# Fewer, larger transposes, one normalisation and a regrouped output projection in a decode attention kernel for two caches

## The chip, the cores and the metric

The kernel runs on one core of one Trainium2 chip. A time is device time of one execution in microseconds (us). The span of a profile runs from the first to the last instruction and is about 1.8 us shorter than the time. The kernel before takes 2564.32 us (median of 3 runs, 2564.31 to 2564.78).

## The reference, cut to what matters

Two independent attention layers, A and B, each decode one token for 8 sequences with 32 heads of 128. Everything is bf16.

```python
B, Sq, D = 8, 1, 1024
H, Sk, Dh = 32, 4096, 128
q = (x @ wq)...                                  # (B, H, 1, Dh)
scores = einsum("bhqd,bhkd->bhqk", q, k_cache) * Dh ** -0.5
o = einsum("bhqk,bhkd->bhqd", softmax(scores), v_cache)
out = o... @ wo                                  # (B, 1, D); A and B side by side
```

Each query meets its own keys and values once, so every byte of the caches is used in one small product. Each of the four caches has 268 MB, and each of the four weight matrices 8.4 MB.

## The kernel before

One tile is 8 heads of one sequence: 128 partitions of 64 KB, 8.39 MB. There are 132 of them: 64 of keys, 64 of values, two of wq and two of wo. They go through a ring of three buffers, all on SyncE's queue:

```python
plan = [("wq", 0, 1), ("k", 0, 0), ("wq", 1, 2)]          # kind, number, buffer
for n in range(NQ - 1):
    plan.append(("k", n + 1, (n + 1) % 2))
    plan.append(("v", n, 2))
plan += [("v", NQ - 1, NQ % 2), ("wo", 0, 2), ("wo", 1, (NQ - 1) % 2)]
```

For every key tile VectorE multiplies by the query (four pieces) and folds, TensorE and VectorE finish the sums, ScalarE makes the exponentials, VectorE spreads them into `PM`, and TensorE multiplies `PM` by the value tile.

The head of the kernel computes q. ScalarE copies eight pieces of it out of PSUM; they are transposed in four rounds of 8 rows, and each round is copied by VectorE:

```python
for hb in range(HB):                                      # 4 rounds
    rows = slice(32 * hb, 32 * hb + B)
    def emit(e, rows=rows):
        for j in range(HQ):
            i = e.transpose(misc_bf16[:, j * B:(j + 1) * B], q_sb[rows, c, j * Dh:(j + 1) * Dh], ident[rows, rows],
                            tile_position=(rows.start, 0))
        return i
    op = add("pe", emit, [opQs[(c, hb, 0)], opQs[(c, hb, 1)], ...])
    ... = add("dve", lambda e, hb=hb: e.tensor_copy(qT..., misc_bf16...), [op])
```

The tail multiplies by wo. The second wo comes in four pieces, so that TensorE can begin before the last has landed:

```python
wo_cuts = ((0, 12), (12, 24), (24, H - 2), (H - 2, H))    # rows r of the second wo
nt = NT if c == NC - 1 else NT // 2                       # column tiles: 2 of 512 for A, 4 of 256 for B
...
for r in range(r0, r1):
    for q in range(nt):
        col = r * D + q * dt
        x = e.matmul(proj[32 * q:32 * q + B, 0:dt], on_sb[:, c, r, :], w[:, col:col + dt],
                     start=(r == 0), stop=(r == H - 1), tile_position=(0, 32 * q))
...
opEv[c] = add("dve", lambda e: e.tensor_copy(orow[0:rows, 0:dt], proj[0:rows, 0:dt]), [opProj[c]] + outs)
for q in range(nt):                                       # B: four stores, two on each of two queues
    outs.append(dma(out[:, 0, c * D + q * dt:c * D + (q + 1) * dt], orow[32 * q:32 * q + B, 0:dt],
                    ("out", 0), [opEv[c]], "sp" if q % 2 == 0 else "act"))
```

Of the kernel before, what the change touches and what calls it, by code (L numbers as in the profile page):

```python
# [4 lines left out]
ACTF = mybir.ActivationFunctionType  # L5
ALU = mybir.AluOpType
AX = mybir.AxisListType
BF16 = mybir.dt.bfloat16
FP32 = mybir.dt.float32
# [130 lines left out]
def _build_kernel(nc, caches, out):  # L140
    B, Sq, D = caches[0][0].shape
    _, H, Sk, Dh = caches[0][1].shape
    NC = len(caches)
# [3 lines left out]
    HQ = 8  # L147
# [7 lines left out]
    RG = T // 4 // 4  # L155
    PH = 128 // H
    MB = HQ * PH
    NT = 4
    DT = D // NT

    es = ExitStack()
    with es:
# [19 lines left out]
        PM = sb("PM", [128, T, HQ], BF16)  # L182
        accS = sb("accS", [128, 512], BF16)
        o_sb = sb("o_sb", [128, NC * B * H], FP32)
        rl = sb("rl", [128, B], FP32)
        on_sb = sb("on_sb", [128, NC, H, B], BF16)
        orow = sb("orow", [128, 2 * DT], BF16)
        q_sb = PM[:].rearrange("p t j -> p (t j)").rearrange("p (c n) -> p c n", c=NC)

        red_ps = [ps(f"red{i}", 16 * CT) for i in range(2)]  # L190
# [4 lines left out]
        q_ps = [o_ps, pv_ps]  # L195
        misc_bf16 = misc.bitcast(BF16)

        wo_cuts = ((0, 12), (12, 24), (24, H - 2), (H - 2, H))
        sems = {e: es.enter_context(nc.semaphore(f"c_{e}")) for e in ENGINES[1:]}
        for name, n in (("t", 3), ("w", len(wo_cuts)), ("x", 1), ("out", 1)):  # L200
            for i in range(n):
# [5 lines left out]
        def dma(out_ap, in_ap, key, deps, eng="sp"):  # L207
            return add(eng, lambda e: e.dma_start(out_ap, in_ap), deps, dma_key=key)
# [10 lines left out]
        c_own = pool_select(own_m[:], MP - 1, [[MP, HQ], [0, PH]], c_own, ALU.is_ge, 0.0, -1)  # L219
        own = own_m[:, :, 0]  # L220

        c_E = add("pool", lambda e: e.memset(E[:], 0.0))
        for q in range(4):
            c_E = pool_select(E[:, :, PH - 1:].rearrange("p i (j u) -> p i j u", u=PH)[:, :, :, 0], -32 * q, [[-8, 4], [-1, HQ]], c_E)
        c_oh = add("dve", lambda e: e.tensor_copy(own_h[:], own), [c_own])
        c_half = add("dve", lambda e: e.tensor_reduce(half[:], own.rearrange("p (g i) -> p i g", i=2), AX.X, ALU.add), [c_own])
        c_half = add("dve", lambda e: e.tensor_scalar(half[:], half[:], 1e30, -1e30, ALU.mult, ALU.add), [c_half])
        c_proj = add("dve", lambda e: e.memset(proj[:], 0.0))

        opT, opMul, opEacc, opRed, opNgm, opExp = {}, {}, {}, {}, {}, {}  # L230
        opPV, opAcc, opExt, opSt, opQb, opQbc, opQ, opQs, opQT = {}, {}, {}, {}, {}, {}, {}, {}, {}
# [24 lines left out]
        def load_tiles():  # L256
            while issued[0] < len(plan):
                kind, n, w = plan[issued[0]]
                prev = before[issued[0]]
                dep = opUse.get(prev)  # L260
                if prev is not None and dep is None:
                    return
                to, key = ring[:, w, :], ("t", w)
                if kind in ("k", "v"):
                    c, b, hb = where(n)
                    from_ = caches[c][1 if kind == "k" else 2][b, hb * HQ:(hb + 1) * HQ].rearrange("u (m t) d -> (u m) (t d)", m=MP)
                    opT[(kind, n)] = dma(to, from_, key, [dep])
                elif kind == "wq":
                    opT[(kind, n)] = dma(to[:, 0:DC * H * Dh], caches[n][3].rearrange("(p k) n -> p (k n)", k=DC), key, [dep])
                else:  # L270
                    from_ = caches[n][4].rearrange("(p r) n -> p (r n)", r=H)
                    for i, (r0, r1) in enumerate(wo_cuts if n == NC - 1 else ((0, H),)):
                        opT[(kind, n, i)] = dma(to[:, r0 * D:r1 * D], from_[:, r0 * D:r1 * D], key if n < NC - 1 else ("w", i), [dep])
                issued[0] += 1


        def make_q(c):
            w = tile_of("wq", c)
            for f in range(2):
                def emit(e, f=f):  # L280
                    for k in range(DC):
                        for hb in range(HB):
                            col = k * H * Dh + (2 * hb + f) * 512
                            i = e.matmul(q_ps[f][32 * hb:32 * hb + B, :], xT[:, (c * DC + k) * B:(c * DC + k + 1) * B],
                                         w[:, col:col + 512], start=(k == 0), stop=(k == DC - 1), tile_position=(0, 32 * hb))
                    return i
                opQ[(c, f)] = add("pe", emit, [c_xT, opT[("wq", c)]] + [opQs.get((c - 1, hb, f)) for hb in range(HB)])
                for hb in range(HB):
                    rows = slice(32 * hb, 32 * hb + B)
                    opQs[(c, hb, f)] = add("act", lambda e, rows=rows, f=f: e.activation(q_sb[rows, c, f * 512:(f + 1) * 512], q_ps[f][rows, :], ACTF.Copy),  # L290
                                           [opQ[(c, f)]])
            opUse[("wq", c)] = opQ[(c, 1)]

        def make_qT(c):
            for hb in range(HB):
                rows = slice(32 * hb, 32 * hb + B)

                def emit(e, rows=rows):
                    for j in range(HQ):
                        i = e.transpose(misc_bf16[:, j * B:(j + 1) * B], q_sb[rows, c, j * Dh:(j + 1) * Dh], ident[rows, rows],  # L300
                                        tile_position=(rows.start, 0))
                    return i
                op = add("pe", emit, [opQs[(c, hb, 0)], opQs[(c, hb, 1)], c_ident, c_xT, opQT.get("last"), opQbc.get(0), opQbc.get(1)])
                opQT[c] = opQT["last"] = add("dve", lambda e, hb=hb: e.tensor_copy(  # L304
                    qT[:, c].rearrange("p (b h) -> p h b", h=H)[:, hb * HQ:(hb + 1) * HQ, :],
                    misc_bf16[:, 0:HQ * B].rearrange("p (j b) -> p j b", b=B)), [op])

        def make_stage(n):
            def emit(e, at):
# [95 lines left out]
                          [opExt[n]], moves=True)  # L405


        def make_norm(c):
            ns = range(c * HB * B, (c + 1) * HB * B)

            def emit(e):
                for hb in range(HB):
                    x = e.matmul(misc[MB * hb:MB * (hb + 1), 0:B], own_m[:].rearrange("p j u -> p (j u)"),
                                 rsum[:].rearrange("p (n h) -> p h n", h=HB)[:, hb, c * B:(c + 1) * B], start=True, stop=True, tile_position=(0, MB * hb))
                return x
            ls = add("pe", emit, [opExp[ns[-1]], c_own, opQbc[NQ - 1], opNorm.get(c - 1)])
            rec = add("dve", lambda e: e.reciprocal(rl[:], misc[:, 0:B]), [ls, opNorm.get(c - 1)])
            opNorm[c] = add("dve", lambda e: e.tensor_tensor(
                on_sb[:, c].rearrange("p r b -> p b r"), o_sb[:, c * B * H:(c + 1) * B * H].rearrange("p (b r) -> p b r", b=B),
                rl[:].unsqueeze(2).to_broadcast([128, B, H]), ALU.mult), [rec, opOc[ns[-1]]])  # L420

        def make_proj(c):
            w = tile_of("wo", c)

            nt = NT if c == NC - 1 else NT // 2
            dt = D // nt
            for i, (r0, r1) in enumerate(wo_cuts if c == NC - 1 else ((0, H),)):
                def emit(e, r0=r0, r1=r1):
                    for r in range(r0, r1):
                        for q in range(nt):  # L430
                            col = r * D + q * dt
                            x = e.matmul(proj[32 * q:32 * q + B, 0:dt], on_sb[:, c, r, :], w[:, col:col + dt],  # L432
                                         start=(r == 0), stop=(r == H - 1), tile_position=(0, 32 * q))
                    return x
                opProj[c] = add("pe", emit, [opNorm[c], opT[("wo", c, i)], c_proj, opEv.get(c - 1)])
            rows = 32 * (nt - 1) + B
            opEv[c] = add("dve", lambda e: e.tensor_copy(orow[0:rows, 0:dt], proj[0:rows, 0:dt]), [opProj[c]] + outs)  # L437
            for q in range(nt):
                outs.append(dma(out[:, 0, c * D + q * dt:c * D + (q + 1) * dt], orow[32 * q:32 * q + B, 0:dt],
                                ("out", 0), [opEv[c]], "sp" if q % 2 == 0 else "act"))  # L440


        x_sb = ring[0:B, 2, 0:NC * D].rearrange("p (c d) -> p c d", c=NC)
        op_x = [dma(x_sb[:, c, :], caches[c][0].rearrange("b s d -> b (s d)"), ("x", 0), [c_oh], "act") for c in range(NC)]

        def emit_xT(e):
            for c in range(NC):
                for k in range(DC):
                    col = (c * DC + k) * B
                    i = e.transpose(misc_bf16[:, col:col + B], x_sb[:, c, :].rearrange("b (p k) -> b k p", k=DC)[:, k, :],  # L450
                                    ident[0:B, 0:B])
            return i
        op_xT = opUse[("x", 0)] = add("pe", emit_xT, [c_ident, op_x[-1]])
        load_tiles()
# [37 lines left out]
        make_red(NS - 1)  # L492
        make_shift(n)
        make_pm(n)
        make_norm(0)
        make_pv(n, 0, RG)
        make_acc(n)
        load_tiles()
        make_ext(n)
        make_norm(1)  # L500
        make_proj(0)
        make_proj(1)
        assert issued[0] == len(plan)
# [3 lines left out]
            o.token = (("x", 0), 16 * NC)  # L507
        loops = {"pe": (1, 2, (NQ - 2) // 2), "dve": (3, 2, (NQ - 4) // 2), "act": (3, HB, (NQ - 4) // HB)}

        P.run("sp", nc.sync, sems, part=(0, 2))  # L510
        block = es.enter_context(nc.Block())

        @block.sync
        def _(eng):
            P.run("sp", eng, sems, part=(2, None))
            eng.wait_ge(sems[("out", 0)], counts[("out", 0)])

        @block.tensor
        def _(eng):
# [10 lines left out]
        @block.gpsimd  # L530
        def _(eng):
            P.run("pool", eng, sems)


def bass_concat_heads__mha_block_cached__mha_block_cached__decode_kernel(
# [32 lines left out]
```

## Time and profile before

| what | before |
|---|---|
| time, median of 3 | 2564.32 us |
| span of the profile | 2563.2 us |
| bytes moved | 1107.49 MB |
| busy: TensorE, VectorE, ScalarE | 44%, 85%, 5% |

These are lines of the page. The rows of digits show the busy share of 40 slices of the span, in tenths; the line after the rate is the chain of waits that ended last, by engine; the last line is the costliest group of VectorE, where the figures after the bar are busy time, mean ns of one instruction, and idle time before them with what ended it.

```profile
span 2563.2 us, 18707 instructions
PE 1122.2 (44%) x7648; PEld 395.1 (15%) x7648; DVE 2173.1 (85%) x1043; ACT 130.0 (5%) x401; POOL 2.6 (0%) x14
...
DVE  3898898898898898898898888888988988988983
...
DMA  9999999999999999999999999999999999999999
...
HBM read 1107.33 MB, written 0.03 MB: 432 GB/s over the span
...
DMA 52%; DVE 28%; issue 16%; PE 4%; another core or an unknown queue 0%; ACT 0%; DVEq 0%; SPq 0%
...
L329 DVE TENSOR_TENSOR ring<-ring,qbc 128x8192 bf16<-128x8192 bf16 x256 | 1131.8, 4421 | 311.3 <-DMA ring<-in_A_k_cache_dram 153.5
```

The DMA row shows 9, 90% or more, in all 40 slices: the load stream runs through, at 432 GB/s over the span. VectorE is nearly as busy, and the chain of waits spends 28% on it, but it waits 311.3 us in all for key tiles: 4.9 us for each of 64.

The head, from the timeline: start, duration, engine, operation, and in brackets the idle time before it and what ended that. "SPq" and "ACTq" lines are DMA issues.

```profile
1.27 0.42 SPq L208 DMA_DIRECT2D ring<-in_A_k_cache_dram  x1
...
2.29 0.17 DVE L225 CAST own_h<-own_m 128x8 bf16<-128x8 f32 x1 [2.29 <-POOL own_m L212]
...
3.12 0.29 ACTq L208 DMA_DIRECT2D ring<-in_B_x_dram  x1
...
29.31 2.43 ACT L290 ACTIVATE PM<-pv 8x512 bf16<-8x512 f32 x4
...
29.95 0.35 PE L300 MATMUL misc<-ident,PM 8*128 8x8 bf16 x8 [0.92 <-ACT PM L290]
30.34 0.43 DVE L304 COPY qT<-misc 128x64 bf16<-128x64 bf16 x1 [13.00 <-PE misc L300]
...
33.24 0.43 DVE L304 COPY qT<-misc 128x64 bf16<-128x64 bf16 x1 [0.53 <-PE misc L300]
...
34.40 0.28 ACT L318 ACTIVATE qbc<-misc 128x128 bf16<-128x128 f32 x1 [0.38 <-PE misc L316]
...
43.72 4.42 DVE L329 TENSOR_TENSOR ring<-ring,qbc 128x8192 bf16<-128x8192 bf16 x1 [10.04 <-DMA ring<-in_A_k_cache_dram]
```

The first query is ready at 34.68 us, and VectorE then waits until 43.7 us for the first key tile. The first rounds of transposes start at 29.95.

The tail, from the timeline:

```profile
2549.49 1.48 PE L432 MATMUL proj<-ring,on_sb 128*8 128x256 bf16 x48 [0.78 <-DVE orow L437]
2555.12 2.73 PE L432 MATMUL proj<-ring,on_sb 128*8 128x256 bf16 x48 [4.14 <-DMA ring<-in_B_wo_dram]
2558.61 1.88 PE L432 MATMUL proj<-ring,on_sb 128*8 128x256 bf16 x32 [0.76 <-DMA ring<-in_B_wo_dram]
2560.54 0.42 DVE L437 CAST orow<-proj 104x256 bf16<-104x256 f32 x1 [11.11 <-PE proj L432]
2560.99 0.63 SPq L208 DMA_DIRECT2D out_dram<-orow  x2
```

One stretch of it by window; after the busy times come TensorE's granted clock, the DMA share and the rate:

```profile
2558.00:2560.00 2.00, 1.39 (x28) 0.78 (x32) 0.00 (x0) 0.00 (x0) 0.00 (x0) 0.50 0.25 100
```

The clock is at half here. TensorE had idled 4.14 us between the first two pieces of the second wo, and in that time the clock fell: it was 1.00 from 2545 to 2552 us and from 2553.0 to 2553.5, and 0.50 from 2554 us on. The same 48 matmuls took 1.48 us in the first piece and 2.73 us in the second. The last piece landed at 2559.8 us, and 3.4 us later the kernel ended.

### The profile page before, as it was taken

What the parts mean: (1) busy time and instruction counts of PE and PEld (TensorE: products, weight loads), DVE (VectorE), ACT (ScalarE), POOL (GpSimd) and SP (SyncE); (2) the same over time, 40 slices, a digit from 0 to 9 for tenths busy, and PEclk for the clock granted to TensorE, in tenths of its full rate; (3) what the DMA queues carried; (4) which work ended last, traced back from release to release, by engine and by line L of the source; (5) the groups of instructions that cost most, each with busy time, mean ns of one, the idle gap of its engine ahead of it and who ended that gap; (6) DMA issues with size and microseconds to landing.
All of it is one profiled execution on the core that took longest, in us unless ns stands there. A gap on an engine that the chain in (4) does not pass through costs nothing.

```text
span 2563.2 us, 18707 instructions
## 1 busy us (share of the span) xinstructions
PE 1122.2 (44%) x7648; PEld 395.1 (15%) x7648; DVE 2173.1 (85%) x1043; ACT 130.0 (5%) x401; POOL 2.6 (0%) x14
## 2 busy tenths in 40 slices
PE   2443443443444444444444444443434444434435
PEld 1111111111111111111111111111111111111112
DVE  3898898898898898898898888888988988988983
ACT  1100000000000000000000000000000000000000
POOL 0000000000000000000000000000000000000000
PEclk7666675766667676766767666767767667666667
DMA  9999999999999999999999999999999999999999
GB/s 425 427 438 430 437 431 437 431 437 431 436 432 436 431 437 430 438 430 438 430 438 429 438 430 438 429 437 431 437 431 436 432 436 432 434 433 434 433 435 391
DMA packets 19577, 1107.49 MB, mean 432 GB/s; under 512 B 2224, under 2 KB 2272, under 8 KB 2416
## 3 DMA queue, kind: packets, MB, share of 16 engines
q1 hardware_dynamic: 19488, 1107.32, 99.9%
q8 instruction: 6, 0.10, 0.0%
q10 hardware_dynamic: 80, 0.05, 0.0%
q14 instruction: 3, 0.02, 0.0%
HBM read 1107.33 MB, written 0.03 MB: 432 GB/s over the span
## 4 chain that ended last, share of the span: by engine, by line
DMA 52%; DVE 28%; issue 16%; PE 4%; another core or an unknown queue 0%; ACT 0%; DVEq 0%; SPq 0%
DMA ring<-in_A_k_cache_dram 25%; DMA ring<-in_B_k_cache_dram 25%; DVE ring L329 10%; DVE ring L334 10%; PE red L344 4%; DVE s_sb L352 4%; DVE PM L369 3%; DMA ring<-in_B_wo_dram 1%; DVE rmax L358 1%; DVE rtmp L359 0%; ACT PM L290 0%; DVEq L135 0%; DVE ngm L362 0%; PE proj L432 0%
## 5 line engine op out<-in xcount | busy, mean ns | idle before, releaser
L329 DVE TENSOR_TENSOR ring<-ring,qbc 128x8192 bf16<-128x8192 bf16 x256 | 1131.8, 4421 | 311.3 <-DMA ring<-in_A_k_cache_dram 153.5
L344 PE MATMUL red<-ring,ident 128*128 128x512 bf16 x2048 | 784.0, 552 | 1390.3 <-DVE ring L334 1390.3
L334 DVE TENSOR_TENSOR ring<-ring 128x4096 bf16<-128x4096 bf16 x256 | 582.4, 2275 | 0.0
L344 PEld LDWEIGHTS red<-ring,ident 128*128 128x128 bf16 x2048 | 240.1, 128 | 1842.3 <-DVE ring L334 1492.9
L352 DVE TENSOR_REDUCE s_sb<-red 128x64 f32<-128x1024 f32 x256 | 312.1, 1219 | 3.7 <-PE red L344 3.7
L381 PE MATMUL pv<-ring,PM 128*32 128x512 bf16 x4096 | 274.8, 416 | 4.7 <-DVE PM L369 4.7
L369 DVE TENSOR_TENSOR PM<-pe,own_h 128x2048 bf16<-128x2048 bf16 x64 | 146.2, 2285 | 0.7 <-ACT pe L364 0.7
L381 PEld LDWEIGHTS pv<-ring,PM 128*32 128x32 bf16 x4096 | 104.2, 104 | 188.9 <-issue 116.7
L318 ACT ACTIVATE qbc<-misc 128x128 bf16<-128x128 f32 x64 | 17.8, 278 | 1093.7 <-PE misc L316 1093.7
L364 ACT ACTIVATE pe<-s_sb,ngm 128x256 bf16<-128x256 f32 x64 | 32.6, 509 | 467.4 <-DVE ngm L362 467.4
L389 ACT ACTIVATE accS<-pv 128x512 bf16<-128x512 f32 x64 | 38.2, 597 | 351.2 <-PE pv L381 351.2
L398 PEld LDWEIGHTS o<-accS,E 128*32 128x32 bf16 x1024 | 31.3, 100 | 49.6 <-issue 48.4
L398 PE MATMUL o<-accS,E 128*32 128x32 bf16 x1024 | 38.1, 185 | 0.7 <-ACT accS L389 0.7
L404 ACT ACTIVATE o_sb<-o 32x32 f32 (+1 forms) x64 | 11.9, 186 | 453.4 <-PE o L398 445.3
L358 DVE TENSOR_REDUCE rmax<-s_sb 128x1 f32<-128x256 f32 x64 | 26.9, 420 | 2.2
L437 DVE CAST orow<-proj 40x512 bf16<-40x512 f32 (+1 forms) x2 | 1.1, 554 | 26.1 <-PE proj L432 26.1
L432 PE MATMUL proj<-ring,on_sb 128*8 128x256 bf16 (+1 forms) x192 | 14.8, 387 | 13.6 <-DMA ring<-in_A_wo_dram 7.9
L311 ACT ACTIVATE qst<-qT 128x128 bf16 (+1 forms) x64 | 18.8, 293 | 2.0 <-DVE qT L304 2.0
L304 DVE COPY qT<-misc 128x64 bf16<-128x64 bf16 x8 | 3.5, 436 | 17.2 <-PE misc L300 17.2
L359 DVE TENSOR_SCALAR rtmp<-half,rmax 128x32 f32<-128x32 f32 x64 | 15.5, 241 | 2.3
L362 DVE TRANSPOSE_TENSOR_REDUCE ngm<-rtmp 128x1 f32<-128x32 f32 x64 | 13.6, 212 | 2.2
L316 PE MATMUL misc<-ident,qst 128*128 128x128 bf16 x64 | 14.8, 232 | 0.9 <-ACT qst L311 0.9
(33 smaller groups left out, 63.6 us busy)
## 6 DMA issues: line engine op xcount, KB each, us to landing
ring<-in_B_wo_dram SPq DMA_DIRECT2D x2, 3072.0 KB, 31.4
ring<-in_B_wo_dram SPq DMA_DIRECT2D x1, 1536.0 KB, 38.1
ring<-in_A_k_cache_dram SPq DMA_DIRECT2D x32, 39.9
ring<-in_A_v_cache_dram SPq DMA_DIRECT2D x32, 27.8
ring<-in_B_k_cache_dram SPq DMA_DIRECT2D x32, 39.9
ring<-in_B_v_cache_dram SPq DMA_DIRECT2D x32, 27.8
ring<-in_B_wo_dram SPq DMA_DIRECT2D x1, 512.0 KB, 38.9
out_dram<-orow SPq DMA_DIRECT2D x2, 4.0 KB
```

Of the source, the lines that this page charges most:

```text
L311: return e.activation(qst[:, n % 2, :].rearrange("p (j m) -> p j m", m=MP), from_.unsqueeze(2).to_broadcast([128, HQ, MP]), ACTF.Copy)
L318: opQbc[n] = add("act", lambda e: e.activation(qbc[:, n % 2, :], misc[:, 0:Dh], ACTF.Copy), [opQb[n], _at(opMul, NR * (n - 2) + NR - 1)])
L329: opMul[s] = add("dve", lambda e: e.tensor_tensor(v, v, qbc[:, n % 2, :].unsqueeze(1).to_broadcast([128, CT, Dh]), ALU.mult), [opT[("k", n ...
L334: return add("dve", lambda e: e.tensor_tensor(v[:, :, 0:64], v[:, :, 0:64], v[:, :, 64:128], ALU.add), [opMul[s]])
L344: i = e.matmul(dst, ident[:], v[:, g, :, j, :], start=(j == 0), stop=(j == 3))
L352: opRed[s] = add("dve", lambda e: e.tensor_reduce(s_sb[:, n % 2, r * CT:(r + 1) * CT], red_ps[s % 2][:, :].rearrange("p (t w) -> p t w", w ...
L358: m = add("dve", lambda e: e.tensor_reduce(rmax[:], s_sb[:, n % 2, :], AX.X, ALU.max), [opRed[NR * n + NR - 1]])
L364: opExp[n] = add("act", lambda e, at: e.activation(pe[:], s_sb[:, n % 2, :], ACTF.Exp, bias=ngm[:, n % 2:n % 2 + 1], scale=scale, accum_ou ...
L369: opPM[n] = add("dve", lambda e: e.tensor_tensor(PM[:], pe[:].unsqueeze(2).to_broadcast([128, T, HQ]), own_h[:].unsqueeze(1).to_broadcast( ...
L381: i = e.matmul(pv_ps[32 * q:32 * (q + 1), :], PM[:, t:t + 4, :].rearrange("p t j -> p (t j)"), v[:, t * Dh:(t + 4) * Dh], start=(g == 0), ...
L389: opAcc[n] = add("act", lambda e: e.activation(accS[:], pv_ps[:], ACTF.Copy), [opPV[n], _at(opExt, n - 1)])
L398: x = e.matmul(to, E[:, i, PH - 1 - u:PH - 1 - u + MB], accS[:, i * 128 + H * u:i * 128 + H * (u + 1)], start=(i == 0 and u == 0), stop=(i ...
```

## The change

Its intent is to shorten both ends: fewer and larger transposes, one normalisation, TensorE kept busy in the tail, two engines for the last eviction and one store on each queue. The core of the diff, with cuts:

```diff
-    NT = 4
+    NT = 2
...
-        wo_cuts = ((0, 12), (12, 24), (24, H - 2), (H - 2, H))
+        wo_cuts = ((0, 18), (18, 26), (26, H - 2), (H - 2, H))
...
+        c_PM = add("pool", lambda e: e.memset(PM[:], 0.0))
         c_E = add("pool", lambda e: e.memset(E[:], 0.0))
...
-                dep = opUse.get(prev)
+                dep = c_oh if (kind, n) == ("k", 0) else opUse.get(prev)
...
-            for hb in range(HB):
-                rows = slice(32 * hb, 32 * hb + B)
...
+            rows = 32 * (HB - 1) + B
+            def emit(e):
+                for j in range(HQ):
+                    i = e.transpose(misc_bf16[:, j * 128:j * 128 + rows], q_sb[0:rows, c, j * Dh:(j + 1) * Dh], ident[0:rows, 0:rows])
+                return i
+            op = add("pe", emit, [opQs[(c, hb, f)] for hb in range(HB) for f in range(2)] + ...)
...                                # one VectorE copy of 256 columns; one normalisation for both caches
+            for q in range(NT):
+                rows = slice(32 * q, 32 * q + B)
+                eng = ("dve", "act")[q % 2]          # one tile evicted by VectorE, the other by ScalarE
...
+            for q in range(NT):
+                outs.append(dma(..., ("out", 0), [opEv[c][q]], ("sp", "act")[q % 2]))
...
-        P.run("sp", nc.sync, sems, part=(0, 2))
+        P.run("sp", nc.sync, sems, part=(0, 1))
...                                # the wait for the stores moves from SyncE to GpSimd
```

The transposes of x become 8 of 16 rows instead of 16 of 8. The new `c_PM` exists because a transpose of 104 rows also reads the rows between the groups of 8, which the copies of q leave unwritten.

More of the change, by code (lines that the diff above doesn't have):

```diff
@@ L184, in _build_kernel @@
         o_sb = sb("o_sb", [128, NC * B * H], FP32)
-        rl = sb("rl", [128, B], FP32)
+        rl = sb("rl", [128, NC * B], FP32)
         on_sb = sb("on_sb", [128, NC, H, B], BF16)
-        orow = sb("orow", [128, 2 * DT], BF16)
+        orow = sb("orow", [128, DT], BF16)
         q_sb = PM[:].rearrange("p t j -> p (t j)").rearrange("p (c n) -> p c n", c=NC)
@@ L227, in _build_kernel @@
         c_half = add("dve", lambda e: e.tensor_scalar(half[:], half[:], 1e30, -1e30, ALU.mult, ALU.add), [c_half])
-        c_proj = add("dve", lambda e: e.memset(proj[:], 0.0))
         opT, opMul, opEacc, opRed, opNgm, opExp = {}, {}, {}, {}, {}, {}
@@ L283, in emit @@
                             col = k * H * Dh + (2 * hb + f) * 512
-                            i = e.matmul(q_ps[f][32 * hb:32 * hb + B, :], xT[:, (c * DC + k) * B:(c * DC + k + 1) * B],
+                            i = e.matmul(q_ps[f][32 * hb:32 * hb + B, :], xT[:, (k * NC + c) * B:(k * NC + c + 1) * B],
                                          w[:, col:col + 512], start=(k == 0), stop=(k == DC - 1), tile_position=(0, 32 * hb))
@@ L290, in make_q @@
                     opQs[(c, hb, f)] = add("act", lambda e, rows=rows, f=f: e.activation(q_sb[rows, c, f * 512:(f + 1) * 512], q_ps[f][rows, :], ACTF.Copy),
-                                           [opQ[(c, f)]])
+                                           [opQ[(c, f)], c_PM])
             opUse[("wq", c)] = opQ[(c, 1)]
         def make_qT(c):
-            for hb in range(HB):
-                rows = slice(32 * hb, 32 * hb + B)
-                def emit(e, rows=rows):
-                    for j in range(HQ):
-                        i = e.transpose(misc_bf16[:, j * B:(j + 1) * B], q_sb[rows, c, j * Dh:(j + 1) * Dh], ident[rows, rows],
-                                        tile_position=(rows.start, 0))
-                    return i
-                op = add("pe", emit, [opQs[(c, hb, 0)], opQs[(c, hb, 1)], c_ident, c_xT, opQT.get("last"), opQbc.get(0), opQbc.get(1)])
-                opQT[c] = opQT["last"] = add("dve", lambda e, hb=hb: e.tensor_copy(
-                    qT[:, c].rearrange("p (b h) -> p h b", h=H)[:, hb * HQ:(hb + 1) * HQ, :],
-                    misc_bf16[:, 0:HQ * B].rearrange("p (j b) -> p j b", b=B)), [op])
+            rows = 32 * (HB - 1) + B
[3 more added lines that the diff above has]
+                return i
+            op = add("pe", emit, [opQs[(c, hb, f)] for hb in range(HB) for f in range(2)]
+                     + [c_ident, c_xT, opQT.get("last"), opQbc.get(0), opQbc.get(1)])
+            opQT[c] = opQT["last"] = add("dve", lambda e: e.tensor_copy(
+                qT[:, c].rearrange("p (b g j) -> p j g b", g=HB, j=HQ),
+                misc_bf16[:, 0:HQ * 128].rearrange("p (j g w) -> p j g w", g=HB, w=32)[:, :, :, 0:B]), [op])
         def make_stage(n):
@@ L405, in make_ext, with make_norm @@
                           [opExt[n]], moves=True)
-        def make_norm(c):
-            ns = range(c * HB * B, (c + 1) * HB * B)
+        def make_norm():
             def emit(e):
                 for hb in range(HB):
-                    x = e.matmul(misc[MB * hb:MB * (hb + 1), 0:B], own_m[:].rearrange("p j u -> p (j u)"),
-                                 rsum[:].rearrange("p (n h) -> p h n", h=HB)[:, hb, c * B:(c + 1) * B], start=True, stop=True, tile_position=(0, MB * hb))
-                return x
-            ls = add("pe", emit, [opExp[ns[-1]], c_own, opQbc[NQ - 1], opNorm.get(c - 1)])
-            rec = add("dve", lambda e: e.reciprocal(rl[:], misc[:, 0:B]), [ls, opNorm.get(c - 1)])
-            opNorm[c] = add("dve", lambda e: e.tensor_tensor(
-                on_sb[:, c].rearrange("p r b -> p b r"), o_sb[:, c * B * H:(c + 1) * B * H].rearrange("p (b r) -> p b r", b=B),
-                rl[:].unsqueeze(2).to_broadcast([128, B, H]), ALU.mult), [rec, opOc[ns[-1]]])
+                    x = e.matmul(misc[MB * hb:MB * (hb + 1), 0:NC * B], own_m[:].rearrange("p j u -> p (j u)"),
+                                 rsum[:].rearrange("p (n h) -> p h n", h=HB)[:, hb, :], start=True, stop=True, tile_position=(0, MB * hb))
+                return x
+            ls = add("pe", emit, [opExp[NQ - 1], c_own, opQbc[NQ - 1]])
+            rec = add("dve", lambda e: e.reciprocal(rl[:], misc[:, 0:NC * B]), [ls])
+            return add("dve", lambda e: e.tensor_tensor(
+                on_sb[:].rearrange("p c r b -> p c b r"), o_sb[:].rearrange("p (c b r) -> p c b r", c=NC, b=B),
+                rl[:].rearrange("p (c b) -> p c b", c=NC).unsqueeze(3).to_broadcast([128, NC, B, H]), ALU.mult), [rec, opOc[NQ - 1]])
         def make_proj(c):
             w = tile_of("wo", c)
-            nt = NT if c == NC - 1 else NT // 2
-            dt = D // nt
             for i, (r0, r1) in enumerate(wo_cuts if c == NC - 1 else ((0, H),)):
@@ L429, in emit @@
                     for r in range(r0, r1):
-                        for q in range(nt):
-                            col = r * D + q * dt
-                            x = e.matmul(proj[32 * q:32 * q + B, 0:dt], on_sb[:, c, r, :], w[:, col:col + dt],
+                        for q in range(NT):
+                            col = r * D + q * DT
+                            x = e.matmul(proj[32 * q:32 * q + B, :], on_sb[:, c, r, :], w[:, col:col + DT],
                                          start=(r == 0), stop=(r == H - 1), tile_position=(0, 32 * q))
@@ L434, in emit @@
                     return x
-                opProj[c] = add("pe", emit, [opNorm[c], opT[("wo", c, i)], c_proj, opEv.get(c - 1)])
-            rows = 32 * (nt - 1) + B
-            opEv[c] = add("dve", lambda e: e.tensor_copy(orow[0:rows, 0:dt], proj[0:rows, 0:dt]), [opProj[c]] + outs)
-            for q in range(nt):
-                outs.append(dma(out[:, 0, c * D + q * dt:c * D + (q + 1) * dt], orow[32 * q:32 * q + B, 0:dt],
-                                ("out", 0), [opEv[c]], "sp" if q % 2 == 0 else "act"))
@@ L443, in _build_kernel @@
-        x_sb = ring[0:B, 2, 0:NC * D].rearrange("p (c d) -> p c d", c=NC)
-        op_x = [dma(x_sb[:, c, :], caches[c][0].rearrange("b s d -> b (s d)"), ("x", 0), [c_oh], "act") for c in range(NC)]
-        def emit_xT(e):
-            for c in range(NC):
-                for k in range(DC):
-                    col = (c * DC + k) * B
-                    i = e.transpose(misc_bf16[:, col:col + B], x_sb[:, c, :].rearrange("b (p k) -> b k p", k=DC)[:, k, :],
-                                    ident[0:B, 0:B])
+                opProj[c] = add("pe", emit, [c_norm, opT[("wo", c, i)]] + opEv.get(c - 1, []))
@@ new lines, in make_proj @@
+            opEv[c] = []
+            for q in range(NT):
+                rows = slice(32 * q, 32 * q + B)
+                eng = ("dve", "act")[q % 2]
+                if eng == "dve":
+                    op = add("dve", lambda e, rows=rows: e.tensor_copy(orow[rows, :], proj[rows, :]), [opProj[c]] + outs)
+                else:
+                    op = add("act", lambda e, rows=rows: e.activation(orow[rows, :], proj[rows, :], ACTF.Copy), [opProj[c]] + outs)
+                opEv[c].append(op)
@@ new lines, in make_proj @@
+            for q in range(NT):
+                outs.append(dma(out[:, 0, c * D + q * DT:c * D + (q + 1) * DT], orow[32 * q:32 * q + B, :],
+                                ("out", 0), [opEv[c][q]], ("sp", "act")[q % 2]))
+        x_sb = ring[0:NC * B, 2, 0:D]
+        op_x = [dma(x_sb[c * B:(c + 1) * B, :], caches[c][0].rearrange("b s d -> b (s d)"), ("x", 0), [c_oh], "act") for c in range(NC)]
+        def emit_xT(e):
+            for k in range(DC):
+                i = e.transpose(misc_bf16[:, k * NC * B:(k + 1) * NC * B], x_sb.rearrange("b (p k) -> b k p", k=DC)[:, k, :],
+                                ident[0:NC * B, 0:NC * B])
@@ L494, in _build_kernel @@
         make_pm(n)
-        make_norm(0)
         make_pv(n, 0, RG)
@@ L499, in _build_kernel @@
         make_ext(n)
-        make_norm(1)
+        c_norm = make_norm()
         make_proj(0)
@@ L514, in _ @@
         def _(eng):
-            P.run("sp", eng, sems, part=(2, None))
-            eng.wait_ge(sems[("out", 0)], counts[("out", 0)])
+            P.run("sp", eng, sems, part=(1, None))
         @block.tensor
@@ L532, in _ @@
             P.run("pool", eng, sems)
+            eng.wait_ge(sems[("out", 0)], counts[("out", 0)])
 def bass_concat_heads__mha_block_cached__mha_block_cached__decode_kernel(
```

## The prediction

> **What bounds the kernel now.** The load stream. The page shows the 16 DMA engines nine tenths busy in all 40 slices, 1107.5 MB at a mean of 432 GB/s, with VectorE at 85% and TensorE at 44%. From the chain of waits, the first key tile lands at 43.70 us and the last at 2481.95 us; 126 tiles of 8.39 MB land in between, so one tile costs 19.35 us (433.5 GB/s). [...] 132 tiles x 19.35 us = 2554 us. The rest of the 2563.2 us span is about 5 us at the head, and 3.4 us after the last wo piece lands (2559.8 us). Only those ends can change, and the bytes don't.
>
> **Head.** The four rounds of 8-row transposes and 0.43 us copies (29.95 to 33.67 us, and again near 76 us) become one round: 8 transposes of 104 rows and one copy of 256 elements, estimated at 1.5 us instead of 3.7. Twice about 2.2 us saved, and half of the 16 x transposes (about 0.5 us). None is on the critical path: the first query is ready at 34.7 us, its key tile lands at 43.7 us; and at 72.7 to 82 us a key tile is still arriving with a value tile queued behind it. Holding the first key load back to about 2.5 us (from 1.27) starves nothing, as wq occupies the stream until 23 us; x may land earlier than 15.97 us, worth nothing either. The added clearing of PM on GpSimd (a few us) ends long before 26.9 us, when it is needed. Head: 0, within 0.5 us.
>
> **Steady state.** Untouched: 0.
>
> **Tail.** One normalisation of 512 columns (estimated 2.6 us, from 1.3 us for 256) runs from about 2532.3 to 2535.1 us, before the first wo tile lands at 2540.0: free. The first piece of the second wo grows from 12 to 18 rows and arrives about 2551.2 instead of 2547.3, so TensorE idles less after the first projection (2548.7). In the trace its clock falls to half at about 2553.6, after that idle. [...] Two tiles of 512 take 0.42 us a row cold and 0.22 warm (first projection); four of 256 took 0.23 cold. If it stays warm, or rewarms in the 18 rows, the last matmuls end near 2560.4 (before 2560.5), since the last piece still lands near 2559.8. If cold, 0.5 to 1.8 us later. The eviction goes from 0.42 us to 0.59 (ScalarE, as its 8x512 copies) or 0.68 (VectorE): +0.25. One store a queue instead of two: -0.33. [...] Tail: -0.2, between -0.7 and +1.8.
>
> **Prediction.** 2564.1 us, 8 in 10 between 2562.6 and 2565.4. Faster by over 2%: 0.005; within 2%: 0.99; slower by over 2%: 0.005.
>
> **What would show it.** Tile period 19.35 us unchanged; last wo piece landing within 0.5 us of 2559.8; the q copies done 2 us sooner with the first key multiply still released by its DMA at 43.7; proj matmuls of the last pieces at 0.22 us a row with clock 1.0; evictions of 0.6 to 0.7 us; one store each on two queues; about 3.2 us from landing to end.
>
> **What would make it wrong.** TensorE cold at the end; a changed stream rate [...]; the first key load delayed enough to leave the stream empty; run-to-run drift, since the effect is smaller than a tenth of a per cent.

Passages of it are cut, each marked: two comparisons with figures that no trace of this case shows, a list of causes that could have changed the stream's rate, and a term of the tail's sum for which no trace had a number. The tail came to -0.2 us in all: +0.25 for the eviction, -0.33 for the stores, the rest the term that is cut. With 0 for the head and for the steady state, the 2564.32 us of before less 0.2 give the 2564.1 us.

## More of the kernel before

The chain alternates between DMA and VectorE because each load waits for a buffer that VectorE's work has freed. That is no proof that VectorE costs time. A load can be issued late and still find the loads ahead of it unfinished.

## The result, and the profile after

| what | before | after |
|---|---|---|
| time, median of 6 | 2564.48 us | 2564.52 us |
| lowest to highest | 2564.31 to 2564.78 | 2564.34 to 2564.73 |
| span of the profile | 2563.2 us | 2562.5 us |

The ratio is 1.0000, with a 95% interval of 0.9987 to 1.0013.

The same lines of the page, after:

```profile
span 2562.5 us, 18439 instructions
PE 1120.6 (44%) x7520; PEld 391.4 (15%) x7520; DVE 2172.9 (85%) x1034; ACT 130.9 (5%) x403; POOL 4.3 (0%) x15
...
HBM read 1107.33 MB, written 0.03 MB: 432 GB/s over the span
...
L328 DVE TENSOR_TENSOR ring<-ring,qbc 128x8192 bf16<-128x8192 bf16 x256 | 1131.1, 4418 | 310.5 <-DMA ring<-in_A_k_cache_dram 157.3
```

There are 128 fewer matmuls, the same bytes at the same rate, and the same wait for key tiles (310.5 us). The head, from the timeline:

```profile
2.20 1.80 POOL L222 MEMSET PM<- 128x2048 bf16 x1
2.28 1.90 DVE L226 CAST own_h<-own_m 128x8 bf16<-128x8 f32 x1 [2.28 <-POOL own_m L212]
...
4.20 0.35 SPq L208 DMA_DIRECT2D ring<-in_A_k_cache_dram  x1
...
31.51 0.88 PE L299 MATMUL misc<-ident,PM 104*128 104x104 bf16 x8 [2.59 <-ACT PM L290]
32.43 1.27 DVE L303 COPY qT<-misc 128x256 bf16<-128x256 bf16 x1 [13.40 <-PE misc L299]
...
34.42 0.28 ACT L317 ACTIVATE qbc<-misc 128x128 bf16<-128x128 f32 x1 [0.38 <-PE misc L315]
...
42.20 4.43 DVE L328 TENSOR_TENSOR ring<-ring,qbc 128x8192 bf16<-128x8192 bf16 x1 [8.50 <-DMA ring<-in_A_k_cache_dram]
```

Two things differ from what had been expected. The small cast took 1.90 us instead of 0.17, and so the first key load was issued at 4.20 us instead of 1.27. And the first query is ready at 34.70 us, no sooner than before. (In the profiles of the runs below with the same round of transposes it is ready between 34.16 and 35.08 us, and at 34.88 us in a second profile of the kernel before.) Neither matters: VectorE still waits 8.5 us for the key tile.

The tail, from the timeline, and the same stretch by window:

```profile
2555.61 1.89 PE L426 MATMUL proj<-ring,on_sb 128*8 128x512 bf16 x16 [0.84 <-DMA ring<-in_B_wo_dram]
2558.11 1.03 PE L426 MATMUL proj<-ring,on_sb 128*8 128x512 bf16 x8 [0.60 <-DMA ring<-in_B_wo_dram]
2559.32 0.60 PE L426 MATMUL proj<-ring,on_sb 128*8 128x512 bf16 x4 [0.18 <-DMA ring<-in_B_wo_dram]
2559.96 0.59 ACT L438 ACTIVATE orow<-proj 8x512 bf16<-8x512 f32 x1 [10.68 <-PE proj L426]
2559.96 0.68 DVE L436 CAST orow<-proj 8x512 bf16<-8x512 f32 x1 [10.59 <-PE proj L426]
...
2560.67 0.30 SPq L208 DMA_DIRECT2D out_dram<-orow  x1
```

```profile
2558.00:2560.00 2.00, 1.63 (x12) 0.37 (x12) 0.04 (x1) 0.04 (x1) 0.00 (x0) 1.00 0.14 54
```

The clock is now full, as intended (1.00 from 2545 to 2562 us). The last piece landed at 2559.27 us and the kernel ended 3.26 us later, against 3.38 us before.

### The profile page after: what moved, and what is told of

It is laid out like the page before. It is cut to its first block, busy times and chain, and to the rows that moved or that the text cites. A ratio compares the mean times of both kernels' runs of the same rounds, so it can differ in the third digit from the quotient of the medians. Undisturbed runs are those within 1.5% of the kernel's fastest.

```text
span 2562.5 us, 18439 instructions
## 1 busy us (share of the span) xinstructions
PE 1120.6 (44%) x7520; PEld 391.4 (15%) x7520; DVE 2172.9 (85%) x1034; ACT 130.9 (5%) x403; POOL 4.3 (0%) x15
## 4 chain that ended last, share of the span: by engine, by line
DMA 51%; DVE 28%; issue 16%; PE 4%; another core or an unknown queue 0%; ACT 0%; DVEq 0%; SPq 0%; POOL 0%; POOLq 0%
DMA ring<-in_A_k_cache_dram 25%; DMA ring<-in_B_k_cache_dram 25%; DVE ring L328 10%; DVE ring L333 10%; PE red L343 4%; DVE s_sb L351 4%; DVE PM L368 3%; DMA ring<-in_B_wo_dram 2%; DVE rmax L357 1%; DVE rtmp L358 0%; ACT PM L290 0%; DVEq L135 0%; PE o L284 0%; DVE ngm L361 0%
## 5 line engine op out<-in xcount | busy, mean ns | idle before, releaser
L328 DVE TENSOR_TENSOR ring<-ring,qbc 128x8192 bf16<-128x8192 bf16 x256 | 1131.1, 4418 | 310.5 <-DMA ring<-in_A_k_cache_dram 157.3
L426 PE MATMUL proj<-ring,on_sb 128*8 128x512 bf16 x128 | 16.4, 411 | 11.7 <-DMA ring<-in_A_wo_dram 8.0
```

What stands on the lines that cost most here:

```text
L328: opMul[s] = add("dve", lambda e: e.tensor_tensor(v, v, qbc[:, n % 2, :].unsqueeze(1).to_broadcast([128, CT, Dh]), ALU.mult), [opT[("k", n ...
```

## The experiments

Twelve kernels ran, all but the first edits of the changed kernel. The theory: the load stream alone sets the time, from its start to the landing of the last piece; of all the other work only what follows that landing is on the path. The rival: VectorE or the head is on the path too (28% of the chain of waits), and the change gained and lost there in equal parts.

### The kernel before once more

No edit.

> The kernel before, unchanged, as a second sample of it. Theory: the 0.7 us by which the profiled spans differ (2563.2 before, 2562.5 after) is mostly where the load stream happened to end; the spans of these runs should scatter by about 0.4 us as the six of the changed kernel do (2562.5 to 2562.9), and from the last wo piece's landing to the end it should take 3.3 to 3.5 us again, against 3.2 in the changed kernel. Rival: the change really shortens the span by 0.7 us; then all spans here are 2563.1 or more.

It took 2564.88 us (4 runs), with 2564.62 us for the kernel before in the same rounds: a ratio of 1.0001 of a kernel to itself. The spans of its four runs were 2562.9 to 2563.1 us, and those of the 32 runs of the kernel before in this and the later rounds were 2562.5 to 2563.2, with a mean of all 36 of 2562.89. The six spans of the changed kernel were 2562.5 to 2562.9, with a mean of 2562.75. So most of the 0.7 us between the two profiles was chance: about 0.14 us of it is left, well inside the scatter of single runs. From the last landing (2559.73 us) to the end it took 3.40 us, as in the first profile (3.38).

### Fewer bytes

```diff
+                    if kind == "v" and n % 4 == 2:
+                        cut = T * Dh * 7 // 8
+                        to, from_ = to[:, 0:cut], from_[:, 0:cut]
                     opT[(kind, n)] = dma(to, from_, key, [dep])
```

> The changed kernel, with 16 of the 64 value tiles loaded only to 7/8 (the rest of the tile is an older tile's data, so the result is wrong on purpose). Stream theory: an eighth of a tile is 19.35 / 8 = 2.42 us, 16 of them 38.7 us, all of it gained: 2525.8 us, within 2 us. Rival, VectorE bounds it (85% busy, 28% of the chain of waits): 2564, or a part of the 38.7 us only.

2526.27 us, against 2564.62 for the kernel before in the same rounds: 38.35 us less, of 38.7 expected (the result is wrong). Every byte taken off the stream came back at the stream's price, though VectorE's work was the same.

### More work for VectorE, below and above its idle time

`PM` is written twice, or four times, for each key tile:

```diff
-            opPM[n] = add("dve", lambda e: e.tensor_tensor(PM[:], ...), [...])
+            for _ in range(2):                            # 4 in the second of these runs
+                opPM[n] = add("dve", lambda e: e.tensor_tensor(PM[:], ...), more)
+                more = [opPM[n]]
```

> The changed kernel with the PM multiply done twice for every key tile: 2.28 us more of VectorE each, 64 times 146 us in all. Stream theory: VectorE has about 4.8 us of idle time before each key tile lands, so nothing changes: 2564.5 us, within 1 us, and that idle time falls to about 2.5 us. Rival, VectorE's 28% of the chain is worth its length: up to 2710 us.

> The changed kernel with the PM multiply done four times for every key tile: 6.85 us more of VectorE each. Stream theory: this exceeds the 4.8 us of idle time by about 2 us, so VectorE becomes the bound and the time grows by about 64 x 2.0 = 130 us, to 2690 us (2670 to 2730). Rival, VectorE bounds already: 64 x 6.85 = 438 us more, 3000 us.

With one extra write, 2564.64 us: no change, for 146 us more work. With three, 2699.21 us (one run, state unknown): 134.6 us more than the kernel before. VectorE's costliest group shows why. First one extra write:

```profile
L328 DVE TENSOR_TENSOR ring<-ring,qbc 128x8192 bf16<-128x8192 bf16 x256 | 1131.1, 4418 | 165.8 <-DMA ring<-in_A_k_cache_dram 86.9 <-DMA ring<-in_B_k_cache_dram 78.9
```

and then three:

```profile
L328 DVE TENSOR_TENSOR ring<-ring,qbc 128x8192 bf16<-128x8192 bf16 x256 | 1130.5, 4416 | 13.9 <-DMA ring<-in_A_k_cache_dram 13.9
```

The wait for key tiles fell from 310.5 us to 165.8, and then to 13.9. Up to that point the extra work is free; past it, VectorE's 2607.4 us of work sets the time. So VectorE's 28% of the chain of waits was worth nothing, and there is a measured limit to that: 4.9 us for each key tile. (The three writes add 6.85 us a tile and cost 134.6 / 64 = 2.1, so about 4.75 us of them were free.)

### GpSimd's clearing, moved

```diff
-        c_PM = add("pool", lambda e: e.memset(PM[:], 0.0))
         c_E = add("pool", lambda e: e.memset(E[:], 0.0))
...
+        c_PM = add("pool", lambda e: e.memset(PM[:], 0.0))
```

> The changed kernel with one move: GpSimd clears PM after it has built E, not before. Theory: VectorE's cast of own_h was held (1.90 us instead of 0.17) by the long GpSimd write that had started 0.1 us before it; now it runs beside short ones and takes 0.2 us or less up to 0.4; x and the first key load are issued near 2.6 us instead of 4.2, and x lands 1.5 us sooner (about 16.5). The time stays at 2564.5 us within 0.4, as the stream holds the first wq until 23 us anyway. Rival 1: the cast waits for something else (its first use of VectorE, or the select): it stays 1.9 us. Rival 2: the late issue costs stream time: the kernel becomes 1.5 us faster.

The cast took 0.17 us, the first key load and x were issued at 2.48 us, and x was transposed at 15.69 instead of 18.13 us, 2.4 us sooner where 1.5 had been expected. The time was 2564.49 us against 2564.55 (ratio 1.0000): the late issue cost nothing. First use and the select are ruled out as causes. The first key tile landed at 42.2 us here as well, so its landing 1.5 us sooner than in the first profile of before does not come from the time of issue.

### The same value, made with two inputs

```diff
-        c_oh = add("dve", lambda e: e.tensor_copy(own_h[:], own), [c_own])
+        c_oh = add("dve", lambda e: e.tensor_tensor(own_h[:], own, own, ALU.mult), [c_own])
```

> The changed kernel, GpSimd's order kept, but own_h is made by a product of two inputs (own times own) instead of a one-input cast. [...] this product takes 0.1 to 0.3 us beside the same clearing, and x and the first key load are issued near 2.6 us. If any VectorE instruction is held by a running GpSimd write, it takes 1.9 us again and they are issued at 4.2.

From its timeline:

```profile
2.20 1.80 POOL L222 MEMSET PM<- 128x2048 bf16 x1
2.28 0.17 DVE L226 TENSOR_TENSOR own_h<-own_m 128x8 bf16<-128x8 f32 x1 [2.28 <-POOL own_m L212]
2.37 0.16 DVE L227 TENSOR_REDUCE half<-own_m 128x2 f32<-128x8 f32 x1
...
2.57 1.61 DVE L228 TENSOR_SCALAR half<-half 128x2 f32<-128x2 f32 x1
```

The product took 0.17 us beside the same clearing. The tensor_scalar after it was held instead (1.61 us, until the clearing ended, against 0.17 us in the changed kernel, where it came after the clearing), while the reduction between them was not (0.16 us; behind the held cast of the changed kernel it had taken 1.81 us). So not every instruction of VectorE was held beside this clearing: of those tried, the cast (1.90 us) and the tensor_scalar were, the product and the reduction were not. Why is not shown. The time stayed at 2564.49 us (one run).

### The transposes in two halves

```diff
-            op = add("pe", emit, [opQs[(c, hb, f)] for hb in range(HB) for f in range(2)] + ...)
+            for f in range(2):                            # 4 transposes each, in two PSUM banks
+                ops.append(add("pe", emit, [opQs[(c, hb, f)] for hb in range(HB)] + ...))
+            for f in range(2):
+                last = add("dve", lambda e, js=js, f=f: e.tensor_copy(qT...[:, js], tp[f]...), [ops[f]])
```

> The changed kernel, with the 104-row transposes and their copy in two halves of 4: the first half needs only the first four ScalarE copies of q (done near 29.0 us), and goes to another PSUM bank. Theory: merging gained nothing because the one round must wait for the last of the eight ScalarE copies (31.5 us), where the four rounds of before ran beside them from 29.95; so here only half of the copy (0.65 us of 1.27) and half the transposes remain after 31.5, and the first query (end of the first copy into qbc) is ready near 33.7 instead of 34.7 us. The time does not move (the key tile lands at 42 us). Rival: the 128-column transposes and the strided copy are themselves the cost; then it is ready at 34.5 or later.

The query was ready at 34.12 us, not at 33.7, mostly since ScalarE's copies ended 0.3 us later in this run (31.78 us). Counted from the end of ScalarE's last copy it took 2.3 us, against 3.2 in the changed kernel and 2.9 before. Part of the 3.2 is the time of the transposes: the eight took 0.88 us there, at a granted clock of 0.50 (31.5 to 32.4 us), and 0.54 in the run with the clearing moved, where the query came 2.9 us after the last copy. Over the profiles with the merged round it is 2.84 to 3.24 us, against 2.94 in both of the kernel before. So the merged round lost by waiting for all eight copies what it saved by being one; half of it runs beside them here. The time was 2564.58 us (one run): nothing, as expected.

### The transposes done four times

```diff
+            for _ in range(4):
                 def emit(e):
                     for j in range(HQ): ...
```

> The changed kernel with the round of transposes and the copy done 4 times one after the other: about 6.7 us more before the first query and again before the second cache's. Theory: off the critical path, the first query is then ready near 41.3 us, just before its key tile at 42.2, and the time stays at 2564.5 us within 0.5; the lag near 83 us is made up within two key tiles. Rival, the head is on the path: 6.7 to 13.4 us slower. It bounds what any saving in the head can be worth.

The query was ready at 41.94 us, 7.2 us later. Near 84 us the copies for the second cache held VectorE up; the key tile after that one was again waited for, 2.27 us, at 121.1 us. The time was 2564.40 us against 2564.55 (ratio 0.9999). The whole head can be 7 us slower at no cost, so nothing saved there can show.

### The second wo with the boundaries of before

```diff
-        wo_cuts = ((0, 18), (18, 26), (26, H - 2), (H - 2, H))
+        wo_cuts = ((0, 12), (12, 24), (24, H - 2), (H - 2, H))
```

> The changed kernel with the piece boundaries of before (12, 24, 30, 32) for the second wo. Theory: the first piece arrives near 2547 us, its 12 rows are done by 2552, TensorE then idles about 3 us and its clock falls to half; two tiles of 512 then take 0.42 us a row instead of 0.22, 12 + 6 + 2 rows in the cold state, so the last matmuls end 0.8 to 2 us later than with the new boundaries after the same landing: from last landing to end 4.0 to 5.2 us instead of 3.2, time 2565.3 to 2566.5. Rival, the boundaries do not matter: 3.2 us and 2564.5.

This expectation failed: 2564.68 us against 2564.69 (ratio 0.9999), and 3.3 us from the last landing to the end. The clock stayed at 1.00 in every window from 2550 us on. With two tiles of 512 the 12 rows of the first piece keep TensorE busy for 2.76 us, not 1.48, and it idles only 1.87 us before the second:

```profile
2549.99 2.76 PE L426 MATMUL proj<-ring,on_sb 128*8 128x512 bf16 x24 [0.78 <-DVE orow L436]
2554.62 2.76 PE L426 MATMUL proj<-ring,on_sb 128*8 128x512 bf16 x24 [1.87 <-DMA ring<-in_B_wo_dram]
```

So the shape of the matmuls was enough to keep the clock up here; these boundaries do as well as the new ones.

The length of the idle time alone does not decide. In the run with one extra VectorE write, which has the same tail as the changed kernel, TensorE idled 2.16 us before the first piece of the second wo, against 2.07 us in the changed kernel. Yet there the clock fell: its mean was 0.83 from 2550 to 2552 us and 0.50 from 2552 to 2554, where the changed kernel has 1.00 throughout. So the full clock of the changed kernel does not come with its tail alone. What else decides is not shown here.

### The second wo in one piece

```diff
+        wo_cuts = ((0, H),)
```

> The changed kernel with the second wo in one piece. Theory: work after the last landing is the one part of TensorE's that is on the path, one for one: 32 rows after the landing, about 8 cold (0.42 us) and 24 warm (0.22), 8.7 us instead of 0.62: time 2564.5 + 8.0 = 2572.5 us, within 0.7. Rival: hidden by something else, less than 4 us slower.

2572.69 us, against 2564.52 for the changed kernel: 8.2 us more (8.0 more than the kernel before in the same rounds). TensorE took 9.06 us after the landing instead of 0.60:

```profile
2559.63 9.06 PE L426 MATMUL proj<-ring,on_sb 128*8 128x512 bf16 x64 [10.84 <-DMA ring<-in_B_wo_dram]
```

In the two profiles the stretch from the last landing to the end grew by as much, from 3.26 to 11.77 us. Work after the last landing counts one for one; beside bytes and VectorE's work past its idle time, nothing else did.

(The 8 rows at half clock in the expectation are those of the first projection: in the changed kernel it ran from 2539.85 us, and the clock was 0.50 from 2542 to 2543 us and 1.00 from 2543.5 on, which is about 8 rows of 0.42 us.)

### An attempt to beat both

The last piece has 1 row; the output is made in four tiles of 256 placed so that VectorE and ScalarE each evict half of the columns; GpSimd clears `PM` last:

```diff
+        wo_cuts = ((0, 18), (18, 26), (26, H - 1), (H - 1, H))
...
+                            col = r * D + q % 2 * DT + q // 2 * (DT // 2)        # q in range(4)
...
+            opEv[c] = [add("dve", lambda e: e.tensor_copy(orow[0:n40, 0:h], proj[0:n40, 0:h]), ...),
+                       add("act", lambda e: e.activation(orow[0:n40, h:DT], proj[64:64 + n40, 0:h], ACTF.Copy), ...)]
```

> An attempt to beat both: the changed kernel with GpSimd clearing PM last, the second wo's last piece of 1 row, four column tiles of 256 as before but placed so that VectorE and ScalarE each copy one half of the columns of both output halves (40 rows of 256, 0.42 us and less instead of 0.68), and still one store a queue. Theory: from last landing to end 2.7 us (3.2 in the changed kernel, 3.4 before), so 0.5 us off the span: 2564.0 us, below what the verdict can tell. Rival: the stores wait for the slower of two engines on two semaphores, and nothing is gained.

2564.55 us against 2564.69 (5 runs, ratio 0.9998): no gain, and 3.4 us from the last landing (2559.5 us) to the end. The evictions took 0.42 and 0.38 us, as meant, but TensorE was finished sooner with each piece, idled longer (2.04 us before the last rows, against 0.60 before the last but one piece of the changed kernel), and was at half clock at the end. The window and the last rows from the timeline:

```profile
2558.00:2558.50 0.50, 0.00 (x0) 0.00 (x0) 0.00 (x0) 0.00 (x0) 0.00 (x0) 0.50 0.46 176
```

```profile
2558.91 1.45 PE L427 MATMUL proj<-ring,on_sb 128*8 128x256 bf16 x24 [2.04 <-DMA ring<-in_B_wo_dram]
```

### The same, with TensorE kept busy

```diff
+                            if c < NC - 1 or r < 26:                              # an unused product beside each
+                                e.matmul(misc[32 * q:32 * q + B, 0:DT // 2], on_sb[:, c, r, :], w[:, col:col + DT // 2],
+                                         start=True, stop=True, tile_position=(0, 32 * q))
```

> The previous attempt (four tiles of 256, evictions of 40 rows by 256, a last piece of 1 row), plus a second, unused product beside each of the projections' up to row 26 of the second cache, into an idle PSUM bank, so that TensorE stays busy as long as with two tiles of 512. Theory: the attempt gained nothing since TensorE, done sooner with each piece, idled longer and its clock was 0.50 from 2558 us on: 6 rows took 1.45 us. Kept busy, the clock is 1.0 there, the last 6 rows are done about 0.35 us after the last landing (0.9 in the attempt), and from last landing to end it takes about 2.85 us against 3.2 to 3.3 in the changed kernel: span 2562.4, time 2564.1 us. Rival: the clock is not what held it; then the last rows take 1.4 us again and the span stays at 2562.8.

It was slower: 2567.23 us against 2564.80 (ratio 1.0008, interval 0.9994 to 1.0022; but its five spans were 2564.7 to 2565.7 us, above all of the kernel before). The clock was 1.00 from 2558 us on, but TensorE was late, and after the second stop below it was at half clock for most of the time from 2554 to 2558 us (means of 0.53 and 0.62 in the two halves). The chain of waits shows it standing still with nothing released:

```profile
2545.30 1.66 issue
...
2550.64 2.25 issue
...
2558.99 0.68 issue
```

The DMA view has one packet of the instruction queue (0.02 MB) shortly before each stop: one starts between 2544 and 2545 us, one between 2550.0 and 2550.6, one between 2557.0 and 2558.9. The changed kernel has such packets too, one from 2544 to 2545 us and one from 2556.9 to 2557.0, and no stop. What held TensorE is not shown: no run here tests it. Whether the attempt before would have gained with a full clock therefore stays open. No version that beats both was found.

## Why the prediction was right

The prediction was 2564.1 us, with 2562.6 to 2565.4 as the range and 99% for "within 2%". Measured: 2564.52 us.

- **What bounds it: right.** From the first key tile's landing to the last's it had 19.35 us a tile; after, (2481.66 - 42.18) / 126 = 19.36 us. That is 433 to 434 GB/s. The runs with fewer bytes and with more work for VectorE show the cause rather than argue it: 38.35 us for 38.7 us of bytes, nothing for 146 us of VectorE.
- **Head, worth zero: right, but two steps in it were wrong.** The prediction had one round of transposes "estimated at 1.5 us instead of 3.7" and the q copies done 2 us sooner. The round took 2.2 us (0.88 and 1.27), and it can start only when the last of ScalarE's copies is done, at 31.5 us instead of 29.95, so nothing was left (34.70 against 34.68 us). The step that failed is having costed the operations without their overlap. And the first key load was to be held back "to about 2.5 us"; it went at 4.20, since the added clearing held VectorE's cast. The prediction counted GpSimd's clearing on GpSimd alone. Neither cost anything: the first sat inside 7 us of measured slack, and the run with the clearing moved took the same time.
- **Steady state: right.** Between 100 and 2500 us VectorE is busy for 2097.10 us before and 2096.58 us after, at 433 GB/s both times.
- **Tail: right within what can be seen.** The clock stayed full, the evictions took 0.59 and 0.68 us, there is one store on each queue, and from last landing to end it took 3.26 us instead of 3.38: 0.12 us saved, where 0.2 had been predicted. This repeats: 3.25 to 3.26 us in five more profiles with this tail, 3.40 in the second one of the kernel before. The eviction added 0.26 us and the store issues gave back 0.36 (predicted +0.25 and -0.33); waiting on GpSimd gave nothing that shows. The regrouped matmuls at full clock gave only 0.04 us: the eviction began 0.69 us after the last landing, and 0.73 before, at half clock. The last landing itself moves by more than all this from profile to profile (2559.27 to 2559.81 us). The reason given for the full clock was only half right: the prediction credited the larger first piece, and the run with the old boundaries had a clock of 1.00 with the wider matmuls alone; and the run with one extra VectorE write, where the clock fell with the same tail, shows that the two together do not make sure of it. The fallback in it, that TensorE "rewarms in the 18 rows", was seen there: the clock's means were 0.50 from 2552 to 2554 us, 0.82 from 2554 to 2556 and 1.00 from 2556 on, and from last landing to end it was 3.25 us all the same.

Open: why the first key tile landed at 43.7 and 43.4 us in two profiles of the kernel before, at about 42.2 in most of the changed one, and at about 43.5 in one of them. The second key tile was started at 82.1 to 82.6 us in all four profiles compared, so no time hangs on it.

So where did the expected gain go? It was off the path from the start. The change made the head's work smaller without making it earlier, in a place where a whole 7 us are idle. In the tail it saved 0.12 us, of the 3.4 us that are the tail's whole worth, and 0.12 us is 0.005% of the time.

## What to carry to other kernels

Before shortening a stage, measure its slack by lengthening it: a doubled instruction that costs nothing shows that a halved one gains nothing, and a larger multiple shows where the slack ends. Where a stream of loads runs through (90% or more in all 40 slices) and every engine has idle time left in each tile, as here, only fewer bytes, and the work after the last landing, count; the chain of waits still listed VectorE with 28%, which cost nothing. Merging small steps into one large one also merges their waits, and a small loop that ran beside its producer may have been as fast.
